# Two column tiles of 64 in place of four of 32 for the dense products that precede the products with V

## Chip, cores and metric

The kernel runs on 1 core of one Trainium2 chip. The metric is the device time of one execution in microseconds. TensorE (PE) multiplies, VectorE (DVE), ScalarE (ACT) and GpSimd (POOL) work on the results, SyncE (SP) issues most DMAs.

## The reference

A layer norm of x (2048 tokens, 640 features, bf16) feeds two branches. Branch A is an attention in four segments of 512 tokens, 32 heads of 20, with a memory M and z that each segment reads and then updates. Branch B is a gated unit with 1536 inner features. Cut to what matters:

```python
xn = _layernorm(x)
q, k, v = heads(xn @ wq), heads(xn @ wk), heads(xn @ wv)
for s in range(4):                                   # segments of 512
    p = _softmax(qs @ ks.T * scale + mask)           # causal in the segment
    a_dot = p @ vs
    a_mem = (phi(qs) @ M) / (phi(qs) @ z + 1e-6)
    o = g * a_mem + (1 - g) * a_dot                  # g = sigmoid(beta)
    M = M + phi(ks).T @ vs
    z = z + sum(phi(ks))
A = o @ wo
B = (_sigmoid(xn @ w_gate) * (xn @ w_up)) @ w_down
out = x + A * _silu(B)
```

## The kernel before, in words

The program writes out the order of every engine by hand: instructions run on each engine in the order in which the Python code issues them.

A prologue loads x and weights, keeps PE busy on zeros (`keep_warm_columns`, L638: 17 rounds of four products of 32 columns by 256), normalizes and projects segment 0 and computes the first gate and up products. Then comes the main loop of 80 slots and one more (L907), 20 slots for each segment. A slot does this, in order:

- if the slot is a *visit* (31 of the slots; two in every five, from slot 4 on), `attend_T` (L564) multiplies V by the exponentials of three earlier slots, for four heads: 16 products on L574, four at a time in four column tiles of 32, written to the four quarters of one PSUM tile `ApsT`;
- `scores` (L547) multiplies K by Q for four heads at once, each in its own 32 rows of the array (L550, 23 rows used, 128 columns), into the PSUM tile `Sps`; `exps` (L555) runs the exp of it on ACT (L558) and the causal mask on POOL (L560);
- then dense work fills the slot (`fill`, `step`, L879 to L906): projections of the next segment (`do_K`, `do_Q`, `do_V`, tiles `psq` and `psv`), gate, up and down products (`do_gate`, `do_up`, `do_down`, tiles `gp`, `up`, `yp`), reads of the memory (`mem_part`, tile `am`), the output product (`out_mm`, tile `sp`). A planner gives each slot an equal share by estimated cost; events have due times in slots (`TIMES`).

All this dense work goes through `mm` (L120). It has two forms, chosen slot by slot with `ORDER["columns"] = slot + 1 in visits` (L915). In most slots and in the prologue it is one product of 128 x 128 weights (L124). In the slots just ahead of a visit it is four products of 128 x 32 weights, in four column tiles, with the same streamed operand (L128). Widths are 512 for `gp`, `up` and `psq`, 320 for `yp`, `psv` and `sp`, 147 or 84 for `am`.

Two helpers have products of 32 columns of their own. `m_update` (L380), once for each of segments 1 to 3, issues 80 of them on L390 (63 wide, tile `dm`). `bound_mm` (L329) issues five on L334 (512 wide, tile `cps`), once in the prologue and three times in the loop. In the loop both stand in slots that are just ahead of a visit.

Names of the rows below: PE is a product, PEld the load of its weights; "128*32" is rows by columns of the weights.

Of the kernel before, what the change touches and what calls it, by code (L numbers as in the profile page):

```python
# [15 lines left out]
L = 512  # L16
# [59 lines left out]
def kernel(  # L76
# [43 lines left out]
    def mm(out_, lhsT, rhs, start, stop):  # L120


        if not ORDER["columns"]:
            nc.tensor.matmul(out_, lhsT=lhsT, rhs=rhs, start=start, stop=stop, skip_group_check=True)  # L124
            return
        for r in range(4):
            cols = slice(32 * r, 32 * r + 32)
            nc.tensor.matmul(out_[cols], lhsT=lhsT[:, cols], rhs=rhs, start=start, stop=stop,  # L128
                             tile_position=(0, 32 * r), skip_group_check=True)

    def load_x(n, a=0, b=4, cols=slice(0, D), eng=nc.sync):
        if n not in xt_of:
# [119 lines left out]
    def ln_tiles(n):  # L252
        mv = lnp.tile([P, 4, 2], F32, name="mv")
        rs = lnp.tile([P, 4], F32, name="rs")
        return mv, rs
# [26 lines left out]
    def proj(n, W, c, dst, evac):  # L282
        ps = ps_d.tile([P, L], F32, name="psq", tag="d")
        for k in range(DC):
            mm(ps[:], W[:, k, c * P:(c + 1) * P], xnT_of[n][:, k, :], k == 0, k == DC - 1)
        if evac is nc.scalar:
            nc.scalar.copy(dst, ps[:])
        else:
            nc.vector.tensor_copy(dst, ps[:])
# [56 lines left out]
    def do_V(n, j, half, evac):  # L346
        ps = ps_d.tile([P, HD], F32, name="psv", tag="d")
        for k in range(DC):
            mm(ps[:], xnT_of[n][:, k, j * P:(j + 1) * P], Wv[:, k, half * HD:(half + 1) * HD],
               k == 0, k == DC - 1)  # L350
        dst = V[n % 2][:, j, half * 16:(half + 1) * 16, 0:DH]
        src = ps[:].rearrange("p (h e) -> p h e", e=DH)
        if evac is nc.scalar:
            nc.scalar.copy(dst, src)
        else:
            nc.vector.tensor_copy(dst, src)
# [44 lines left out]
    def mem_part(n, j, half):  # L401
        s = seg[n]
        if s["odot"] is None:
            s["odot"] = stg.tile([P, 4, D], BF, name="odot", tag="oq")
        am = ps_d.tile([P, 16, E1], F32, name="am", tag="d")
        for i, (c, h0, h1) in enumerate(PIECES[half]):
            off = (h0 - HEADS[c][0]) * E1
            mm(am[:, h0 - 16 * half:h1 + 1 - 16 * half, :].rearrange("p h e -> p (h e)"),
               s["qt"][:, c, j * P:(j + 1) * P], Mbd[:, c, off:off + (h1 - h0 + 1) * E1],
               i == 0, i == len(PIECES[half]) - 1)  # L410
        rm = opool.tile([P, 16], F32, name="rm", bufs=3)
        nc.vector.scalar_tensor_tensor(out=rm[:], in0=am[:, :, DH], scalar=1e-6,
                                       in1=ginv[:, 16 * half:16 * half + 16], op0=ALU.add, op1=ALU.mult)
        nc.vector.reciprocal(rm[:], rm[:])
        nc.vector.tensor_tensor(
            s["odot"][:, j, half * HD:(half + 1) * HD].rearrange("p (h e) -> p h e", e=DH),
            am[:, :, 0:DH], rm[:].unsqueeze(2).to_broadcast([P, 16, DH]), op=ALU.mult)
# [220 lines left out]
    def keep_warm_columns(k, n):  # L638
        for _ in range(k):
            for r in range(4):  # L640
                nc.tensor.matmul(wps[32 * r:32 * r + 32, 0:n], lhsT=warm[:, 32 * r:32 * r + 32], rhs=warm[:, 0:n],
                                 start=True, stop=True, tile_position=(0, 32 * r), skip_group_check=True)

    keep_warm_columns(17, L // 2)
    mv, rs = ln_tiles(0)
    new_seg(0)
    xns, sts = {}, {}
# [342 lines left out]
```

## Time and profile before

| what | value |
|---|---|
| time, median of 3 runs | 317.68 us (317.29 to 317.83) |
| profiled execution, its own time | 317.5 us |
| its span, first to last instruction | 315.7 us |
| granted PE clock over the span | 1.0 |
| products on PE in the profile | 4297 |
| weight loads on PE in the profile | 4327 |
| DVE, ACT, POOL instructions | 507, 228, 231 |

The page gives for each engine its busy time; a product's end is modelled, so neighbouring products overlap in it and only their starts are used for differences. A row of the timeline merges instructions of one kind: start, time from the first start to the last end, engine, line, operation, what is written and read, shapes and count. A few records can be missing; the program has 4327 products.

### The profile page before, as it was taken

Reading aid. Unit: us, or ns where it says so; the run is one execution under the profiler, and the core shown is the slowest. Engines: PE = TensorE matmul, PEld = TensorE weight load, DVE = VectorE, ACT = ScalarE, POOL = GpSimd, SP = SyncE. Lnnn points to the kernel's source line nnn. Section 1 sums busy time; section 2 is a strip of 40 time slices with the busy share of each in tenths; the row PEclk is TensorE's granted clock in tenths of the full one; section 3 lists DMA queues with packets and bytes.
Section 4 is the critical chain, followed back from the end, with each engine's and each line's share of the span. In section 5 each row is a group of like instructions: output and inputs, shape, how many; then the busy total and the mean of one; then the engine's idle time right before and its main releaser. Section 6 shows DMA issues by size and latency. Waiting matters only on the chain.

```text
span 315.7 us, 10227 instructions
## 1 busy us (share of the span) xinstructions
PE 307.1 (97%) x4297; PEld 167.5 (53%) x4327; DVE 224.9 (71%) x507; ACT 226.6 (72%) x228; POOL 133.5 (42%) x231
## 2 busy tenths in 40 slices
PE   7999999999999999999999999999999999999995
PEld 4544444665545444654665454545466655444673
DVE  5473455654868988878869989788787776644575
ACT  3724478778798776778897869679897775777730
POOL 2870035535262544435453364444444353525313
PEclk9999999999999999999999999999999999999999
DMA  7984886410742383504953365239524000280202
GB/s 242 375 329 148 282 227 175 127 45 2 209 149 66 101 140 118 129 24 148 263 171 110 115 106 144 67 110 211 175 78 131 19 23 26 79 148 25 86 21 85
DMA packets 55246, 41.27 MB, mean 131 GB/s; under 512 B 25952, under 2 KB 53824, under 8 KB 55200
## 3 DMA queue, kind: packets, MB, share of 16 engines
q1 hardware_dynamic: 52656, 35.87, 41.4%
q10 hardware_dynamic: 2544, 4.75, 4.1%
q8 instruction: 34, 0.56, 0.7%
q14 instruction: 12, 0.10, 0.1%
HBM read 19.98 MB, written 14.73 MB: 110 GB/s over the span
## 4 chain that ended last, share of the span: by engine, by line
PE 95%; DMA 1%; issue 1%; DVE 1%; ACT 1%; SPq 0%; ACTq 0%
PE up L124 11%; PE gp L124 10%; PE yp L124 10%; PE psq L124 10%; PE Sps L550 8%; PE gp L128 6%; PE yp L128 6%; PE up L128 6%; PE ApsT L574 6%; PE psv L124 5%; PE psq L128 4%; PE sp L124 3%; PE sp L128 3%; PE psv L128 2%; PE sp L534 2%; DMA xt<-in_A_x_dram 1%
## 5 line engine op out<-in xcount | busy, mean ns | idle before, releaser
L558 ACT ACTIVATE pt<-Sps 128x2048 bf16<-128x2048 f32 x80 | 150.2, 1878 | 40.6 <-PE Sps L550 39.6
L560 POOL TENSOR_SCALAR_AFFINE_SELECT pt<-pt 128x512 bf16<-128x512 bf16 x128 | 82.5, 660 | 156.6 <-ACT pt L558 153.8
L437 DVE SCALAR_TENSOR_TENSOR hT<-tg,up 128x512 bf16<-128x512 bf16 x48 | 32.6, 678 | 24.0 <-PE up L124 10.0
L124 PE MATMUL up<-xnT,Wu 128*128 128x512 bf16 x146 | 40.3, 380 | 1.4 <-issue 1.1
L124 PE MATMUL gp<-xnT,Wg 128*128 128x512 bf16 x146 | 38.9, 379 | 0.6 <-issue 0.5
L426 ACT ACTIVATE tg<-gp 128x512 bf16<-128x512 f32 x48 | 28.6, 595 | 14.4 <-PE gp L124 10.0
L124 PE MATMUL yp<-Wd,hT 128*128 128x320 bf16 x246 | 38.2, 300 | 0.0
L550 PE MATMUL Sps<-QT,KT 23*128 23x384 bf16 (+3 forms) x512 | 31.9, 301 | 0.1
L124 PEld LDWEIGHTS <-hT 128*128 128x128 bf16 x246 | 22.7, 98 | 11.3 <-issue 3.0
L454 DVE SCALAR_TENSOR_TENSOR aa<-t,yp 128x320 bf16<-128x320 bf16 x32 | 15.3, 478 | 13.9 <-ACT t L453 13.8
L582 DVE STREAM_TRANSPOSE tb<-ApsT 128x512 f32<-128x512 f32 x31 | 22.0, 711 | 4.1 <-PE ApsT L574 4.0
L128 PE MATMUL gp<-xnT,Wg 128*32 128x512 bf16 x352 | 24.4, 380 | 0.0
L574 PE MATMUL ApsT<-pt,V 128*32 128x512 bf16 (+2 forms) x496 | 23.5, 299 | 0.0
L124 PEld LDWEIGHTS <-Wu 128*128 128x128 bf16 x159 | 14.2, 98 | 17.4 <-issue 4.0
L124 PEld LDWEIGHTS <-Wg 128*128 128x128 bf16 x152 | 14.1, 98 | 15.8 <-issue 1.9
L128 PE MATMUL yp<-Wd,hT 128*32 128x320 bf16 x552 | 21.9, 300 | 0.0
L128 PE MATMUL up<-xnT,Wu 128*32 128x512 bf16 x324 | 21.7, 380 | 0.0
L550 PEld LDWEIGHTS <-KT 23*128 23x128 bf16 x512 | 9.2, 92 | 23.5 <-issue 23.4
L594 DVE STREAM_TRANSPOSE obT<-ob 128x256 f32<-128x256 f32 x31 | 13.5, 434 | 11.1 <-POOL ob L591 11.0
L591 POOL TENSOR_TENSOR ob<-tb,rb 128x320 bf16<-128x320 f32 x27 | 19.9, 735 | 2.2
L124 PE MATMUL psq<-xnT,Wq 128*128 128x512 bf16 x82 | 19.4, 379 | 0.2
L124 PE MATMUL psv<-Wv,xnT 128*128 128x320 bf16 x115 | 18.5, 300 | 0.4 <-ACT xnT L670 0.4
(124 smaller groups left out, 442.2 us busy)
## 6 DMA issues: line engine op xcount, KB each, us to landing
KT<-Kd SPq DMA_DIRECT2D x32, 80.0 KB
QT<-Qd SPq DMA_DIRECT2D x32, 80.0 KB
out_dram<-xt SPq DMA_DIRECT2D x14, 160.0 KB
Wg<-in_B_w_gate_dram ACTq DMA_DIRECT2D x1, 1920.0 KB
Wu<-in_B_w_up_dram ACTq DMA_DIRECT2D x1, 1920.0 KB
xt<-in_A_x_dram SPq DMA_DIRECT2D x3, 640.0 KB
Wd<-in_B_w_down_dram SPq DMA_DIRECT2D x1, 1920.0 KB
Od<-odot SPq DMA_DIRECT2D x3, 640.0 KB
```

The lines of the kernel that those rows point to most:

```text
L124: nc.tensor.matmul(out_, lhsT=lhsT, rhs=rhs, start=start, stop=stop, skip_group_check=True)
L128: nc.tensor.matmul(out_[cols], lhsT=lhsT[:, cols], rhs=rhs, start=start, stop=stop, tile_position=(0, 32 * r), skip_group_check=True)
L426: nc.scalar.activation(tg[:], gp[:], ACT.Tanh, scale=0.5)
L437: nc.vector.scalar_tensor_tensor(out=h[:], in0=seg[n]["tg"][:], scalar=1.0, in1=up[:], op0=ALU.add, op1=ALU.mult)
L454: nc.vector.scalar_tensor_tensor(out=s["aa"][j][:, hs], in0=t2[:], scalar=1.0, in1=yp[:], op0=ALU.add, op1=ALU.mult)
L550: nc.tensor.matmul(Sps[:, r, c0:c0 + ncol], lhsT=KT[32 * r:32 * r + DH + 3, g, kb * P:(kb + 1) * P], rhs=QT[32 * r:32 * r + DH + 3, g, q0: ...
L558: nc.scalar.activation(pt[:, :, 0:ntot], Sps[:, :, 0:ntot], ACT.Exp, scale=SCALE)
L560: nc.gpsimd.affine_select(out=pt[:, :, c0:c0 + P], in_=pt[:, :, c0:c0 + P], compare_op=ALU.is_ge, fill=0.0, base=0, pattern=[[0, 4], [1, P ...
L574: nc.tensor.matmul(ps[32 * r:32 * r + 32, q0:L], lhsT=Vflat[n % 2][:, off:off + 32], rhs=t[:, r, c0:c0 + ncol], start=(i == 0), stop=(i == ...
L582: nc.vector.transpose(tb[:].rearrange("p h e -> p (h e)"), ps[:].rearrange("p (a t b) -> p a b t", t=32, b=2))
L591: eng.tensor_tensor(to, of, by, op=ALU.mult)
L594: nc.vector.transpose(s["obT", g // 4][:, g % 4, :].bitcast(F32), ob[:].rearrange("p a e b -> p (a e b)").bitcast(F32))
```

## The change

`mm` cuts a dense product of these slots into two column tiles of 64 where it had four of 32. Everything else that issues products of 32 columns (L574, L390, L334) stays as it is. In the prologue the products on zeros become 34 rounds of 128 columns of stream in place of 17 rounds of 256.

```diff
         if not ORDER["columns"]:
             nc.tensor.matmul(out_, lhsT=lhsT, rhs=rhs, start=start, stop=stop, skip_group_check=True)
             return
-        for r in range(4):
-            cols = slice(32 * r, 32 * r + 32)
+        for r in range(2):
+            cols = slice(64 * r, 64 * r + 64)
             nc.tensor.matmul(out_[cols], lhsT=lhsT[:, cols], rhs=rhs, start=start, stop=stop,
-                             tile_position=(0, 32 * r), skip_group_check=True)
+                             tile_position=(0, 64 * r), skip_group_check=True)
...
-    keep_warm_columns(17, L // 2)
+    keep_warm_columns(34, L // 4)
```

The changed program has 3415 products on PE, and the instruction lists of the other engines hold the same operations in the same order.

## The prediction

> **What bounds the kernel now.** I read the page first, then the waits of TensorE (PE), then its timeline where the width of its products changes. Two lines of the page, busy time and the chain that ended last:
>
> ```profile
> PE 307.1 (97%) x4297; PEld 167.5 (53%) x4327; DVE 224.9 (71%) x507; ACT 226.6 (72%) x228; POOL 133.5 (42%) x231
> ...
> PE 95%; DMA 1%; issue 1%; DVE 1%; ACT 1%; SPq 0%; ACTq 0%
> ```
>
> PE is busy for 97% of the span and is 95% of the chain; the next engine (ACT) has 72%. A busy PE could still hide waits, so the second view is everything that PE waited for (us in total, times, longest):
>
> ```profile
> PE wps L641 <- DVE mn L149: 1.2, 1, 1.2
> PE up L124 <- issue: 1.1, 7, 0.2
> PE gp L124 <- issue: 0.5, 3, 0.2
> PE psv L124 <- ACT xnT L670: 0.4, 1, 0.4
> PE sp L124 <- issue: 0.3, 2, 0.2
> PE pT L665 <- DVE xn L248: 0.3, 1, 0.3
> ```
>
> The three named releasers belong to the first 7 us. After that PE waits for no other engine. What is added to PE's stream between 12 and 306 us is therefore added to the time; what is taken from it is gained.
>
> The third view is PE's timeline. Its durations overlap (a product's end is modelled), so I read only **starts**: from the start of one group to the start of the next is what the first has cost. The first window has plain products of 128 columns, then `cps` of 32 columns (L334), then plain ones again:
>
> ```profile
> 25.41 1.24 PE L124 MATMUL up<-xnT,Wu 128*128 128x512 bf16 x5
> 26.58 0.61 PE L334 MATMUL cps<-aq,ik 128*32 128x512 bf16 x5
> 27.12 0.61 PE L124 MATMUL gp<-xnT,Wg 128*128 128x512 bf16 x2
> ```
>
> The second has dense products of 32 columns (L128) ahead of the products with V (L574, 32 columns too), then the scores (L550, 23 rows), then plain ones:
>
> ```profile
> 48.29 1.25 PE L128 MATMUL gp<-xnT,Wg 128*32 128x512 bf16 x20
> 49.37 0.72 PE L574 MATMUL ApsT<-pt,V 128*32 128x512 bf16 x16
> 50.02 0.40 PE L550 MATMUL Sps<-QT,KT 23*128 23x384 bf16 x8
> 50.35 0.39 PE L124 MATMUL up<-xnT,Wu 128*128 128x512 bf16 x1
> ```
>
> The third has the way into the 32-column form from the scores, and a long run of it:
>
> ```profile
> 52.83 0.40 PE L550 MATMUL Sps<-QT,KT 23*128 23x512 bf16 x4
> 53.16 1.05 PE L128 MATMUL up<-xnT,Wu 128*32 128x512 bf16 x16
> 54.03 2.21 PE L128 MATMUL yp<-Wd,hT 128*32 128x320 bf16 x60
> 56.07 0.72 PE L574 MATMUL ApsT<-pt,V 128*32 128x512 bf16 x16
> ```
>
> **Price of a product.** Four 32-column products make one set, as large as one plain product. 20 of gp: (49.37 - 48.29)/5 = 0.216 us a set of 512. 60 of yp: (56.07 - 54.03)/15 = 0.136 us a set of 320. Both include the step to L574. Single plain products start 216 ns and 136 ns apart too. So the 32-column form costs nothing in the run, and passing from L128 to L574 costs nothing.
>
> **Price of a change of form.** Into `cps`: 26.58 - 25.41 = 1.17 us for 5 products, which need 5 x 0.216 = 1.08; 93 ns over (by the trace's starts in ns). Out of it: 27.12 - 26.58 = 0.54 us for two sets, 0.43; 96 ns over by those starts (309 and 312 ns where 216 is usual). Here only the number of columns changes; the rows stay at 128. At the scores, where the rows change, they give medians of 96 ns (plain to scores, 49 times), 91 ns (back, 49), 99 ns (scores to L128, 31) and 95 ns (L574 to scores, 31). The mechanism seen there: the first weight load of the new form begins only about 310 ns after the last 512-wide start, whereas in a run it begins within 5 ns of the product before.
>
> **The change, part by part.** The order of events does not depend on how `mm` cuts a product. The instruction lists of DVE, ACT, POOL and SP are the same in both programs, names of buffers aside; no wait, DMA or queue is moved. Only PE's list differs.
>
> (1) 1960 products of 32 columns become 980 of 64 (rows of L128: gp 352, up 324, yp 552, psq 180 and 60, psv 180, sp 240, am 48 and 24): 490 sets, of which 229 are 512 wide, 243 are 320 wide and 18 belong to `am`. With set times of 216 and 136 ns in both forms that the trace shows, I take the same for the one between: **0**. The gain cannot be large, since 32 columns run at the plain rate. The loss: two loads of 64 columns ahead of each set. The nearest rows: the 80 products of `dm` (L390, 32 columns, 63 wide) start over 0.63 us, or 8 ns for a load and a product; so a load of 32 columns holds up the stream for at most 8 ns, one twice as wide for perhaps 16, two of them 32 ns, which fits into 136. Where products are narrowest (`am`, 84 and 147 wide, sets 37 and 65 ns apart), I give 0.1 us for all 18 sets; bounds 0 and 0.35 (37 ns more for each of 6 sets, 10 more for each of 12).
>
> (2) New changes of form. By the built program's order, 64 columns now meet 32 columns at: L128 to L574, 30 times (of 31; once `cps` stands between); L128 to `cps` 3 times and back 2; L128 to `dm` 3 times and back 3. **41 in all**, and none of the old changes goes. Bounds for one: 0 (it is a change of tile in the same rows, as between neighbours of one set) and 99 ns (the dearest row). I take 95 ns, between the two rows in which only the columns change, 93 and 96: 41 x 0.095 = **3.9 us**, all in PE's stream. What stands behind each change on PE is the products with V and the scores; the exp on ACT (L558) that needs the scores already sits idle 39.6 us in all until they are there, and its result is used a slot later, so the delay moves with PE and adds nothing of its own.
> On this point the Trainium skill, TensorEngine Tiling, sections Available Configurations and Key Properties, lists 128x64 and 128x32 as separate configurations, and says that changing the mode, not just the tile, drains the engine. By that rule the sum is the 3.9 us above; if the two counted as one mode it would be 0. No row here holds 64 columns.
>
> (3) The first products: 34 rounds of 128 in place of 17 of 256, the same streaming. The last of them start at 4.63 us, 0.21 a round; the transposes wait for DVE at 5.32 with 0.27 us idle ahead. Plain products of 128 there start 107 ns apart with their loads, which is half of 0.21, so 34 rounds end where 17 did: **0**, covered by the 0.27 us. Without that cover it would cost what it is late.
>
> **Sum.** 3.9 + 0.1 + 0 = 4.0 us on the profiled execution's 317.5 (span 315.7 and 1.8 around it): **321.5 us**. The median shown is 317.68 and runs go from 317.29 to 317.83, so 0.2 either way is in the base. With 91 to 99 ns a change (3.7 to 4.1), 0 to 0.35 for `am` and 0.3 for the base, this case spans 320.9 to 322.3.
>
> **Rivals.**
> - *Changes between 64 and 32 columns are free* (not slower). For it: all tiles span 128 rows, and neighbouring tiles of one set start 2 to 4 ns apart. Against: `cps` also keeps the rows and pays 93 and 96. It decides below 16 ns a change (0.64 us over 41). Time 317.5 to 317.7. Chance 0.11.
> - *They cost about half*: loads can go ahead for one half of the columns. Nothing in the rows lies between 10 and 90 ns. 41 x 0.048 = 2.0: 319.5. Chance 0.06.
> - *64-column loads do not hide*: if each takes the 97 ns that the load rows show and the two go one after the other, a set of 320 waits 194 - 136 = 58 ns, 243 times: 14.1 us, and the 18 sets of `am` some 2.5: 317.5 + 3.9 + 16.6 = 338. Against it: four 32-column loads, each shown with the same 97 ns, cost nothing in sets of 37. Chance 0.04.
> - *No load hides at all*: every set shows one load of 97 ns, 490 x 0.097 = 47.5 us, 317.5 + 3.9 + 47.5 = 369. Against it stands that the sets of 32 columns share their rows just so and pay nothing. Chance 0.01.
> The Trainium skill, TensorE: Matmul & The Clock Gate, section Part 3 (The mechanism), would have it so: loads overlap running products only when the row groups differ. The trace of before disagrees for 32 columns, 216 ns a set with a load ahead of every product.
>
> **Numbers.** Forecast 0.78, rivals 0.11, 0.06, 0.04 and 0.01. The range holds the forecast's own span and reaches down to the half price: 319.3 to 322.4. A measurement can tell about 0.2% (0.64 us) from no change. Only the free change gives less: same 0.10, faster 0.02 (if fewer instructions saved more than I see), slower 0.88.
>
> **What would show it.** In the changed profile: L128 sets still 216 and 136 ns apart; from the last L128 start to L574 about 312 ns (512 wide) or 231 (320 wide), where it was 216 and 136; the same around `dm` and `cps`; PE still waiting for nobody after 7 us; the rise spread over 45 to 306 us, some 0.1 us for each visit of L574. Wrong if L574 follows at 216, or if L128 sets themselves lie farther apart.

## The result, and the profile after

The changed kernel takes 322.73 us (median of 4 runs, 321.95 to 323.66), the one before 317.49 us beside it (4 runs, 317.12 to 317.83): a ratio of 1.0167, 95% interval 1.0133 to 1.0200. It is slower, as forecast, by 5.2 us in the medians; the median lies 0.3 us above the range of 319.3 to 322.4. The profiled execution has 322.28 us (span 320.5), 4.8 us more than the one of before (317.5, span 315.7).

Busy time and chain of the page first, then all that PE waited for. They answer to the first two fences of the prediction:

```profile
PE 311.6 (97%) x3385; PEld 168.1 (52%) x3415; DVE 225.5 (70%) x507; ACT 226.7 (71%) x228; POOL 132.9 (41%) x231
...
PE 95%; DMA 2%; issue 1%; ACT 1%; DVE 1%; SPq 0%; ACTq 0%
```

```profile
PE wps L641 <- DVE mn L149: 1.2, 1, 1.2
PE up L124 <- issue: 1.1, 7, 0.2
PE gp L124 <- issue: 0.5, 3, 0.2
PE psv L124 <- ACT xnT L670: 0.5, 1, 0.5
PE pT L665 <- DVE xn L248: 0.5, 1, 0.5
PE sp L124 <- issue: 0.3, 2, 0.2
```

Nothing new is waited for, and the other engines are as busy as before. The lines with "issue" are no waits at all: these two profiles miss 30 products each (4297 of 4327, 3385 of 3415), and where one is missing its place looks idle. The other profile of the changed kernel, that of a2 below, misses none and has no such line. The loss therefore sits between PE's own products, where no view of waits shows it. It shows in the starts. Here are two of the stretches of PE's timeline that the prediction shows:

```profile
48.18 1.25 PE L128 MATMUL gp<-xnT,Wg 128*64 128x512 bf16 x10
49.35 0.73 PE L574 MATMUL ApsT<-pt,V 128*32 128x512 bf16 x16
50.01 0.40 PE L550 MATMUL Sps<-QT,KT 23*128 23x384 bf16 x8
```

```profile
52.82 0.40 PE L550 MATMUL Sps<-QT,KT 23*128 23x512 bf16 x4
53.15 1.05 PE L128 MATMUL up<-xnT,Wu 128*64 128x512 bf16 x8
54.04 2.20 PE L128 MATMUL yp<-Wd,hT 128*64 128x320 bf16 x30
56.17 0.40 PE L574 MATMUL ApsT<-pt,V 128*32 128x512 bf16 x4
```

Five sets of gp up to L574 took 49.35 - 48.18 = 1.17 us where they took 1.08. In the second stretch the row of `up` took 0.89 us (0.87 before), the row of `yp` 2.13 (2.04). Then L574 took 0.66 up to the scores in the first stretch (0.65 before). By the starts in ns these are three terms: **14** in the first set after the entry from the scores, **97** at the change to 32 columns (counted from the first tile of the last set; 93 from its second tile, which starts 4 ns later), **11** in the first set after the change. The runs themselves are unchanged: of 419 steps between sets of 64 columns, the mean excess over the streaming time is 0 ns.

Around `dm` the change costs both ways. Before, then after:

```profile
98.25 0.81 PE L390 MATMUL dm<-V,ktok 128*32 128x63 bf16 x80
98.87 0.41 PE L128 MATMUL gp<-xnT,Wg 128*32 128x512 bf16 x4
```

```profile
98.00 1.03 PE L128 MATMUL gp<-xnT,Wg 128*64 128x512 bf16 x8
98.96 0.82 PE L390 MATMUL dm<-V,ktok 128*32 128x63 bf16 x80
99.71 0.41 PE L128 MATMUL gp<-xnT,Wg 128*64 128x512 bf16 x2
99.95 0.38 PE L128 MATMUL up<-xnT,Wu 128*64 128x512 bf16 x2
```

Four sets of gp take 0.96 us for 0.86, the 80 products of `dm` 0.75 for 0.63 (here the change back to 64 columns is in it), and the set of gp after them 0.24 for 0.22.

The account over 45 to 306 us: 36 changes into 32 columns x (97 + 11) = 3.89; 5 back into 64 x (98 + 24) = 0.61; 31 entries from the scores x 14 = 0.43; together 4.93 us. The start of this execution was 0.13 us earlier, which leaves 4.80; the spans differ by 4.8.

### The profile page after: what moved, and what is told of

Its sections match the earlier page's. It is cut to its first block, busy times and chain, and to the rows that moved or that the text cites. A ratio compares the mean times of both kernels' runs of the same rounds, so it can differ in the third digit from the quotient of the medians.

```text
span 320.5 us, 8403 instructions
## 1 busy us (share of the span) xinstructions
PE 311.6 (97%) x3385; PEld 168.1 (52%) x3415; DVE 225.5 (70%) x507; ACT 226.7 (71%) x228; POOL 132.9 (41%) x231
## 4 chain that ended last, share of the span: by engine, by line
PE 95%; DMA 2%; issue 1%; ACT 1%; DVE 1%; SPq 0%; ACTq 0%
PE up L124 11%; PE gp L124 10%; PE yp L124 10%; PE psq L124 9%; PE Sps L550 8%; PE ApsT L574 6%; PE gp L128 6%; PE yp L128 6%; PE up L128 6%; PE psv L124 5%; PE psq L128 4%; PE sp L124 3%; PE sp L128 3%; PE psv L128 2%; DMA Wv<-in_A_wv_dram 2%; PE sp L534 1%
## 5 line engine op out<-in xcount | busy, mean ns | idle before, releaser
L128 PE MATMUL gp<-xnT,Wg 128*64 128x512 bf16 x176 | 24.0, 381 | 0.0
L574 PE MATMUL ApsT<-pt,V 128*32 128x512 bf16 (+2 forms) x496 | 23.0, 302 | 0.0
L128 PE MATMUL up<-xnT,Wu 128*64 128x512 bf16 x162 | 21.7, 381 | 0.0
L128 PE MATMUL yp<-Wd,hT 128*64 128x320 bf16 x276 | 21.7, 301 | 0.0
```

Of the source, the lines that this page charges most:

```text
L574: nc.tensor.matmul(ps[32 * r:32 * r + 32, q0:L], lhsT=Vflat[n % 2][:, off:off + 32], rhs=t[:, r, c0:c0 + ncol], start=(i == 0), stop=(i == ...
```

## The experiments

Each was timed beside the kernel before on the same chip: that took 317.51 us beside e1 to e4 (18 runs, 317.11 to 319.08) and 317.80 beside e5, e6 and a2 (11 runs, 317.10 to 319.41). The expected times are sums on 317.5. Against the kernel before beside them the losses are 4.6 us in e1, 4.2 in e3, 2.4 in e4, 3.3 in e5, 2.1 in e6 and 4.5 in a2.

### e1: only the tiles of 64

```diff
-    keep_warm_columns(34, L // 4)        # changed kernel
+    keep_warm_columns(17, L // 2)
```

> Only the tiles of 64; the products on zeros at the start stay 17 rounds of 256. Theory A (all of the loss sits at the 41 new changes of form and at the 31 entries into the 64-column form, as the trace of the changed kernel shows: 97 ns and 11 ns a change, 14 ns an entry): 317.5 + 4.8 = 322.3 us, runs within about 0.7 us of each other as those of before. Theory B (the start with 34 rounds of 128 is what puts the median 0.4 us above that sum and spreads the runs over 1.7 us): here about 322.2 with a narrow spread, and the start alone (e2) wide. If the spread of 1.7 us stays here, it is not the start.

Measured: 322.11 us (6 runs, 321.92 to 323.15), ratio 1.0141, interval 1.0119 to 1.0163. The loss is there without the new start. One of the six runs still lies 1.2 us above the lowest, so most of the spread needs no new start.

### e2: only the start

```diff
-    keep_warm_columns(17, L // 2)        # kernel before
+    keep_warm_columns(34, L // 4)
```

> Only the start changed: 34 rounds of 128 on zeros, dense products in tiles of 32 as before. Theory A: 317.5 us, within 0.2% of before, runs within 0.7 us. Theory B: about 317.9, with runs spread from 317.2 to 318.9.

Measured: 317.82 us (12 runs, 317.42 to 319.17), ratio 1.0005, interval 0.9989 to 1.0021: no difference that the measurement can tell. Its spread of 1.75 us is wider than the 0.7 that theory A allowed, but so is that of the kernel before (1.97 us over 18 runs); the spread is not the start's. The 0.4 us of theory B is too small for these medians, which lie 0.3 us apart. The profiled execution shows nothing of it: its span is 315.7 us, as before.

### e3: no column tiles in the dense products

```diff
-        ORDER["columns"] = slot + 1 in visits
+        ORDER["columns"] = False
```

> No column tiles in the dense products at all: 128 columns in every slot, so 41 changes between 128 and 32 columns are added where the changed kernel has 41 between 64 and 32. Theory A (any change of the number of columns costs the same): 41 x 0.108 = 4.4 us, less 31 x 8 ns for cheaper entries from the scores, so +4.2: 321.7 us, 0.6 below the changed kernel. Rival (64-column products are dear by themselves): +0 to +2 us, below 319.5.

Measured: 321.67 us (6 runs, 321.53 to 323.62), ratio 1.0132, interval 1.0108 to 1.0157; 321.7 was expected. The same stretch of its timeline:

```profile
48.16 1.24 PE L124 MATMUL gp<-xnT,Wg 128*128 128x512 bf16 x5
49.34 0.73 PE L574 MATMUL ApsT<-pt,V 128*32 128x512 bf16 x16
50.00 0.40 PE L550 MATMUL Sps<-QT,KT 23*128 23x384 bf16 x8
```

Five plain products take 1.18 us up to L574, and L574 0.66 up to the scores: the same two terms as behind 64 columns. The rival (64 columns are dear by themselves) falls: nearly the whole loss is there without a single product of 64 columns. That 321.7 was met so closely is in part luck. By the starts a change into 32 columns costs 93 + 11 = 104 ns here, not 108, and the entries from the scores are 3 ns dearer than into 32 columns, not 8 cheaper; the starts add up to 4.4 us where 4.2 were expected.

### e4: tiles of 64 in the other slots

```diff
-        for r in range(4):
-            cols = slice(32 * r, 32 * r + 32)
+        for r in range(P // ORDER["columns"]):
+            cols = slice(ORDER["columns"] * r, ORDER["columns"] * (r + 1))
...
-                             tile_position=(0, 32 * r), skip_group_check=True)
+                             tile_position=(0, cols.start), skip_group_check=True)
...
-        ORDER["columns"] = slot + 1 in visits
+        ORDER["columns"] = 32 if slot + 1 in visits else 64 if slot < OLD else False
```

> Tiles of 32 ahead of the products with V as before, but tiles of 64 in place of 128 columns in the other 46 slots of the loop; no change of form is added, about 700 sets run in tiles of 64. Theory A: each entry from the scores 8 ns dearer than into 128 columns, the first set 14 ns dearer: 46 x 0.022 = +1.0 us: 318.5 us; sets of 216 and 136 ns. Rival (64-column sets cost by themselves, 4.8 us over 490 sets, 10 ns each): 700 x 10 ns = +6.9 us: 324.4.

Measured: 319.93 us (7 runs, 318.64 to 321.23), ratio 1.0067, interval 1.0043 to 1.0091. That is 2.4 us where theory A said 1.0 and the rival 6.9; neither number was met. The profiled execution (span 318.2, 2.5 more than before) tells where it went. First a run of 64 columns, then the place where most of the difference arises:

```profile
39.57 0.40 PE L550 MATMUL Sps<-QT,KT 23*128 23x384 bf16 x8
39.90 1.27 PE L128 MATMUL up<-xnT,Wu 128*64 128x512 bf16 x10
41.00 1.25 PE L128 MATMUL gp<-xnT,Wg 128*64 128x512 bf16 x10
42.08 0.81 PE L128 MATMUL up<-xnT,Wu 128*64 128x512 bf16 x6
```

```profile
165.02 0.82 PE L390 MATMUL dm<-V,ktok 128*32 128x63 bf16 x80
166.98 0.59 PE L128 MATMUL yp<-Wd,hT 128*32 128x320 bf16 x12 [1.15 <-issue]
```

After the entry the first five sets take 1.10 us, the next five 1.08: the sets do not cost, so the rival's mechanism falls. By the starts the first set after each of 46 entries is 24 ns over, where the plain form has 10: 46 x 14 = 0.64 us. The entry itself is not dearer than into plain products (88 ns, and 90), against theory A's 8 more. The rest comes at once: 1.34 us behind the 80 products of one `dm`, where PE sat 1.15 us idle for nothing that the profile shows ("issue"), and 0.38 us at 104 us, where a product also waited 0.2 for DVE. 0.64 + 1.34 + 0.38 = 2.4. Whether every run has such a stop is open; the fastest, 318.64, is 1.1 above the kernel before. What causes it was not tried; the last section tells what the trace shows around it.

### e5: the change moved into the dense work

```diff
-        ORDER["columns"] = slot + 1 in visits
+        ORDER["columns"] = 64 if slot + 1 in visits else False
...
+        fill(due - 500)
+        if ORDER["columns"]:
+            ORDER["columns"] = 32
         fill(due)
```

with `mm` as in e4.

> Tiles of 64 in the first part of the slots ahead of a visit, tiles of 32 for about their last 0.5 us where any dense work is left by then: the change of form moves away from the products with V into the dense work (16 times of 31), and 31 changes are added in place of 41, because no return from cps and dm into 64 columns is left. Theory A (every change costs 108 ns wherever it stands, an entry from the scores into 64 columns 14 more): 31 x 0.108 + 31 x 0.014 = 3.8, 317.5 + 3.8 = 321.3 us. Rival (it is the products with V, or those of cps and dm, that start late behind 64 columns): only 15 places left, 15 x 0.108 + 0.4 = 2.0: 319.5.

Measured: 321.11 us (6 runs, 320.98 to 322.74), ratio 1.0111, interval 1.0088 to 1.0134; theory A said 321.3, the rival 319.5. The span is 319.4 us, 3.7 more than before, where theory A has 3.8. One slot whose change stands inside the run of `yp` (18 sets of 64 columns and 4 of 32 merged in one row):

```profile
63.14 0.40 PE L550 MATMUL Sps<-QT,KT 23*128 23x512 bf16 x4
63.46 3.29 PE L128 MATMUL yp<-Wd,hT 128*64 128x320 bf16 x52
66.58 0.72 PE L574 MATMUL ApsT<-pt,V 128*32 128x512 bf16 x16
67.23 0.40 PE L550 MATMUL Sps<-QT,KT 23*128 23x384 bf16 x8
```

The 22 sets need 22 x 0.136 = 2.99 us. They took 3.00 in the kernel before (63.21 to 66.21 us) and take 3.12 here; 14 + 97 + 11 ns are the difference. L574 then takes 0.65 us, as before the change. The products with V do not suffer from 64 columns; whichever product comes first after a change pays, even one of the same dense sum.

### e6: tiles of 64 ahead of every other visit

```diff
-        ORDER["columns"] = slot + 1 in visits
+        ORDER["columns"] = 32 + 32 * (sorted(visits).index(slot + 1) % 2) if slot + 1 in visits else False
```

with `mm` as in e4.

> Tiles of 64 ahead of every other visit (15 slots), of 32 ahead of the rest: 19 changes added in place of 41, 15 entries in place of 31. Theory A: 19 x 0.108 + 15 x 0.014 = 2.3: 319.8 us. If the loss came from anything that the whole kernel shares (the start, the fetching of instructions, the order), it would not fall in this proportion: 2.3 of 4.8.

Measured: 319.86 us (6 runs, 319.54 to 321.03), ratio 1.0068, interval 1.0046 to 1.0090; 319.8 was expected. Just under half of the changes, 19 of 41, cost just under half of the time, 2.1 us against 4.5 in a2. Two visits of one execution, the first behind 32 columns, the second behind 64:

```profile
48.10 1.25 PE L128 MATMUL gp<-xnT,Wg 128*32 128x512 bf16 x20
49.18 0.72 PE L574 MATMUL ApsT<-pt,V 128*32 128x512 bf16 x16
...
53.85 2.20 PE L128 MATMUL yp<-Wd,hT 128*64 128x320 bf16 x30
55.99 0.73 PE L574 MATMUL ApsT<-pt,V 128*32 128x512 bf16 x16
```

1.08 us for five sets (5 x 0.216), and 2.14 for fifteen that need 2.04.

### a2: the changed kernel once more

> The changed kernel once more, beside e5 and e6. Theory A: 317.5 + 4.8 = 322.3 us, as its trace adds up; the 322.73 of four runs then stood high by the scatter that the kernel before has too (317.11 to 319.08 in 18 runs). If the median is 322.7 again, about 0.4 us is in no trace seen so far.

Measured: 322.31 us (4 runs, 322.12 to 322.71), ratio 1.0139, interval 1.0117 to 1.0161, 4.5 us above the kernel before at 317.80. The 322.73 of the first four runs is not met again; the sum of the trace is.

## Why the prediction was right or wrong, point by point

- **What bounds the kernel: right.** PE's list of waits after is that of before, and every ns added between its products reached the end: 4.93 us by the starts, 4.8 in the span.
- **(1) Runs of 64 columns cost nothing: right.** They take 216 and 136 ns a set, with a mean excess of 0 over 419 steps. The 0.1 us for `am` was not needed: its sets stand 64 and 37 ns apart in all forms.
- **(2) 41 new changes: right in number and kind, too small in size.** This is the step that failed: "I take 95 ns, between the two rows in which only the columns change". The gap is as forecast: from the last start of L128 to L574 it is 309 ns behind sets of 512 and, but for one, 229 behind sets of 320, where 312 and 231 were named. But it is not the whole price. The first set after a change into 32 columns is 11 ns longer (24 into 64), so a change costs 108 and 122 ns: 41 of them 4.5 us, not 3.9. The rows of before held that: the two sets of `cps` took 0.54 us, 0.11 over, of which the prediction booked only the 96 ns from the last start to the next. The first plain product behind `cps` holds 11 ns more, for its follower starts after 227 ns and not 216. Both changes together cost 0.21 us there, where 0.19 was taken.
- **Left out altogether:** the 31 entries from the scores. They are not new changes, so nothing was booked for them, but the first set of 64 columns after them takes 24 ns over where the one of 32 takes 10: 0.43 us. No row of before shows it.
- **(3) The start: right.** e2 is within 0.2% of before, and its span is the same.
- **The sum:** 4.0 was forecast, 4.9 came: 0.6 more for the changes, 0.43 for the entries, 0.1 less for `am`. The profiled execution (322.28) and the second median (322.31) lie inside the range; the first median, 322.73, lies above 322.4. The base was given 0.3 us for the scatter, from 317.29 to 317.83; over 29 later runs the kernel before went from 317.10 to 319.41. So two things are short: the sum, by 0.9 us, and the room for scatter. The 0.4 us by which the first median lies above the profiled execution are in no trace, and their cause is open.
- **Rivals.** Free changes, half the price, loads that do not hide: none happened. A change costs 108 ns or more, and the sets of 64 columns cost nothing extra.
- **Loads of 64 columns last longer,** and the only place where that may show is the first set. Here are the weight loads of one operand, first in the kernel before, then in the changed one (behind the first bar: busy us, mean ns of one):

```profile
L128 PEld LDWEIGHTS <-hT 128*32 128x32 bf16 x552 | 14.2, 97 | 5.2 <-issue 1.6
```

```profile
L128 PEld LDWEIGHTS <-hT 128*64 128x64 bf16 x276 | 15.0, 110 | 4.9 <-issue 2.0
```

110 ns against 97 are 13 more, and the first set after an entry is 14 longer. That the one is the cause of the other is argued from these two numbers, not shown.
- **The rule on modes.** The Trainium skill, TensorEngine Tiling, section Key Properties, says that a change of mode, not just of tile, drains the engine; the list in its section Available Configurations has 128x64 and 128x32 apart. The trace agrees on the cost: 93 ns between 64 and 32 columns in e5 within one sum, against 3 to 4 ns between neighbouring tiles of one set. What it shows of the way is that, behind sets of 512, the first load of 32 columns begins 308 ns after the last start of 64 columns, where in the kernel before the loads of L574 began some 2 ns behind a start of L128. That this is a drain no run shows.

## What to carry to other kernels

Count the changes of the array's form in the order of PE's products, and price each from start to start, the first set after it included: here 104 to 122 ns, whether between 128 and 32 columns or between 64 and 32. Here it paid to give work that leads into a stretch of one form that same form, even though it is wide enough for a larger one: 32-column tiles ran at the full rate and saved 30 changes at the visits alone. A busy engine with no waits can still lose time between its instructions; here the list of waits did not show it, and differences of starts did.

## What the runs showed of the hardware

- A single load of 128 columns without column tiles lasts 98 ns, one of 32 columns in a tile 97, one of 64 in a tile 110. All three hide in a run, even where sets start 37 ns apart.
- The instruction queue q8 moves with the number of PE's instructions: 34 packets before, 27 after, 22 in e3, 39 in e4, at 16 KB each. In e4 PE stopped for 1.15 us right after 80 narrow products that start 8 ns apart; one packet took 0.9 to 1.8 us. That the stop was a wait for instructions is not shown: the last packet ahead of it had landed 1.5 us before PE went on (165.45 us, 166.98), the next began at 168.67, and in e2 PE ran on without a stop past a packet that began at 163.94. No run tested it; the cause is open.
- The kernel before varied between 317.10 and 319.41 us over 29 runs. The start alone does not explain it (e2), and no trace of a run at the high end was seen: open.
